# Filling products moved ahead of the second block's query product, and a third buffer for the index numbers

## The chip, the cores and the metric

The kernel runs on one core of a Trainium2 chip. The metric is the device time of one execution in microseconds (us). The core's engines work side by side, each in the order of its own queue: TensorE (PE) multiplies matrices, VectorE (DVE) and ScalarE (ACT) do element-wise work and copies, GpSimd (POOL) does element-wise work and issues the transfers that gather or scatter rows by index, and SyncE (SP) issues most other transfers (DMAs). An engine waits for another one, or for a transfer, at a semaphore.

## The reference

A gated linear attention over 4 batches, 8 heads, 768 tokens and head size 48 feeds a mixture of 8 experts in which every token goes to one expert.

```python
for t in range(S):                                # attention, per batch and head
    state = alpha[:, :, t, :, None] * state + np.einsum('bhd,bhe->bhde', k[:, :, t], v[:, :, t])
    y[:, :, t] = np.einsum('bhd,bhde->bhe', q[:, :, t], state)
...
for s in range(S):                                # experts, per batch; x is y, 384 wide
    fresh_e = int(np.argmax(logits[b, s]))
    if s == 0 or local_gate[b, s] < 0.5:
        e = fresh_e
    else:
        e = prev_e if prev_e >= 0 else fresh_e
    ...
    h = np.maximum(x[b, s] @ w1[e], 0.0)          # w1[e]: 384 x 1024
    out[b, s] = p[e] * (h @ w2[e])                # w2[e]: 1024 x 384
```

## The kernel before

**The attention stage** takes 24 blocks of 128 tokens, two chunks of 64 each, in one loop over `i`. Blocks 0 to 3 are the first blocks of the four batches. For block `i` DVE computes running products of the gate and their reciprocals (`scan1`, `scan2`; the tiles `A` and `sf`), two blocks ahead of use, and POOL multiplies query and key with them. PE multiplies keys with queries (`pm`, into the bank `pz`), transposes the keys (`kt`, tile `kp`, copied to `kk` by ACT), multiplies queries with the state (`qm`, into `py`), keys with values (`um`, into `up`), and masked scores with values (`ym`, onto `py`). DVE masks the scores (`mask`, tile `pq`) and adds up the state (`sums`, tile `st`). The order of the work on each engine is the order in which the code is written, since every call is pinned to it. In iteration `i` PE's order is `pm(i)`, `kt(i)`, transposes of the finished rows of block `i-2`, `qm(i-1)`, `um(i)`, `ym(i-1)`. The query product `qm(i-1)` reads the state that `sums(i-1)` writes, and DVE's order is `sums(i-1)`, `mask(i)`, `scan1(i+2)`, `scan2(i+2)`.

**Filling products** are products of a tile of zeros, `dz`, with itself. Their results are read by nobody. `dense(DN0)` issues 56 ahead of the loop, and `um` issues `DN + DN1 * (i < 2)` into unread columns of `up`, ahead of its own work: eight for block 0 and eight for block 1.

**The expert stage** works in jobs. The last attention blocks run beside the first expert's jobs `a` and `b`; then come seven jobs `r0` to `r6`, one for each other expert by rank, with up to 512 rows in slices of up to 128. A job has a first layer (`gemm1`: eight groups of nine products into the banks of tile `h`; ACT and DVE turn each group into the parts `hh` and `hl`), a second layer (`gemm2`: 24 products a slice into `yp`, scaled by DVE into `yo`), and a scatter of each slice's rows to the output (`store`). Three banks take the groups of `h` in turn, so the fourth group waits until `hl` of the first has been computed. When job n starts, `numbers()` computes for job n+1 the index numbers `ix` of its rows, on DVE, from `pr`, a row of the lists picked by rank; the gathers of job n+1 and its scatters read them. The tile `ix` has two buffers there, so the numbers of job n+1 go where those of job n-1 stood, whose scatters have been issued as its slices were finished.

Of the kernel before, what the change touches and what calls it, by code (L numbers as in the profile page):

```python
# [10 lines left out]
I32 = mybir.dt.int32  # L11
# [44 lines left out]
NL = 5  # L56
NW = 3
DN0 = 56
DN = 0
DN1 = 8  # L60


# [10 lines left out]
def gla_moe(ctx, tc, akq, vw, vn, wg, w1, w2, cst, tok, out):  # L73
# [30 lines left out]
    v_, s_, g_, t_, y_ = (Engine(e) for e in (nc.vector, nc.scalar, nc.gpsimd, nc.tensor, nc.sync))  # L104
# [105 lines left out]
    class Job:  # L210
# [14 lines left out]

        def numbers(self, more=None):

            self.ix = self.sp.tile([128, 2, self.ns], I32, tag="ix", bufs=2, name=f"ix_{self.nm}")
            if callable(self.first):
                self.pr = self.first()  # L230
                v_.tensor_tensor(self.ix, self.pr[:, 1:3, 0:self.ns], back.unsqueeze(2).broadcast_to([128, 2, self.ns]), ALU.add)
            else:
                w = slice(self.first, self.first + self.ns)
                self.pr = lists[:, :, w]
                v_.tensor_tensor(self.ix, self.pr[:, 1:3], back.unsqueeze(2).broadcast_to([128, 2, self.ns]), ALU.add)
# [88 lines left out]
        def store(self, yo, yp, s):  # L324
            P = self.ways[s].stop - self.ways[s].start
            v_.tensor_scalar_mul(yo, yp, self.pr[0:P, 0, s:s + 1])
            apart(outs, g_.indirect_dma_start(out=out, out_offset=bass.IndirectOffsetOnAxis(
                ap=self.ix[0:P, 0, s:s + 1], axis=0), in_=yo, in_offset=None,
                bounds_check=NTOK - 1, oob_is_err=False))
# [5 lines left out]
    with ac:  # L335
# [4 lines left out]
        py = pa.tile([128, 2, 512], F32, tag="y", name="py")  # L340
# [6 lines left out]
        dz = ap.tile([128, 256], F32R, bufs=1, name="dz")  # L347
# [56 lines left out]
        def qm(i):  # L404

            d = blk[i]
            q = d["q"].rearrange("p (h t) -> p h t", h=HP)
            for hp in range(HP):
                for (e, c) in ((0, 0), (1, 1), (0, 1), (1, 0)):
                    if c == 0 and i < G:  # L410
                        continue
                    r = slice(0, 48) if e else slice(64, 112)
                    t_.matmul(py[c * C:(c + 1) * C, e, hp * D:(hp + 1) * D], lhsT=q[r, hp, c * C:(c + 1) * C],
                              rhs=d["s3"][r, c, hp, :], start=(hp == 0), stop=False, skip_group_check=True)
            r = slice(C if i < G else 0, 128)
            s_.copy(seen[r].rearrange("p (e h) -> p e h", e=2), py[r, :, 0:HP * D:D])

        def half(i):
            vt = blk[i]["vt"]
            s_.copy(vt[0:64, 0, :], vt[0:64, 1, :])  # L420
# [35 lines left out]
        def kt(i):  # L456
            k = blk[i]["k"].rearrange("p (h t) -> p h t", h=HP)
            kp = pp.tile([128, HP, R], F32, tag="kp", name=f"kp_{i}")
            for hp in range(HP):
                t_.transpose(kp[:, hp, :], k[:, hp, :], ident[0:R, 0:R])  # L460
            kk = ap.tile([128, HP, R], F32, tag="kk", name=f"kk_{i}")
            s_.copy(kk, kp)
            blk[i]["kk"] = kk

        def pm(i):

            d = blk[i]
            k = d["k"].rearrange("p (h t) -> p h t", h=HP)
            q = d["q"].rearrange("p (h t) -> p h t", h=HP)
            pe = pz  # L470
            for hp in range(HP):
                for (par, c) in ((0, 0), (1, 1), (0, 1), (1, 0)):
                    w = slice(c * C, (c + 1) * C)
                    r = slice(0, 48) if par else slice(64, 112)
                    t_.matmul(pe[c * C:(c + 1) * C, par, hp * C:(hp + 1) * C], lhsT=k[r, hp, w], rhs=q[r, hp, w],
                              start=True, stop=True)
            d["pe"] = pe

        def mask(i):
            d = blk[i]  # L480
            pq = ap.tile([128, 2, HP, C], F32, tag="pq", bufs=2, name=f"pq_{i}")
            v_.tensor_tensor(pq, d["pe"][:, :, 0:HP * C].rearrange("p e (h t) -> p e h t", h=HP),
                             cc("tri")[:, 0:C].unsqueeze(1).unsqueeze(1).broadcast_to([128, 2, HP, C]), ALU.mult)
            d["pq"] = pq

        def state0(i):

            d = blk[i]
            if i < G:
                d["s3"] = ap.tile([R, 3, HP, D], F32, tag="st", bufs=G + 1, name=f"st_{i}")  # L490
            else:
                d["s3"] = st["S", i % G]

        def um(i):

            d = blk[i]
            kk, vt = d["kk"], d["vt"]
            uw = pp.tile([128, 512], F32, tag="up", name=f"up_{i}")
            for _ in range(DN + DN1 * (i < 2)):
                t_.matmul(uw[:, 384:512], lhsT=dz[:, 0:128], rhs=dz[:, 0:128], start=True, stop=True)  # L500
            d["up"] = uw[0:R, 0:2 * CW].rearrange("p (h c d) -> p c h d", c=2, h=HP)
            for hp in range(HP):
                n = slice(2 * hp * D, 2 * (hp + 1) * D)
                t_.matmul(uw[64:112, n], lhsT=kk[:, hp, 64:112], rhs=vt[:, :, 2 * hp * D:(2 * hp + 1) * D],
                          start=True, stop=True)
                t_.matmul(uw[0:64, n], lhsT=kk[:, hp, 0:64], rhs=vt[:, :, (2 * hp + 1) * D:(2 * hp + 2) * D],
                          start=True, stop=True)

        def sums(i):
            d = blk[i]  # L510
            s3 = d["s3"]
            n = 2 if i + G < NB else 1
            if i < G:
                v_.tensor_copy(s3[:, 1:1 + n], d["up"][:, 0:n])
                return
            v_.tensor_tensor(s3[:, 1:1 + n], d["up"][:, 0:n], s3[:, 0].unsqueeze(1).broadcast_to([R, n, HP, D]), ALU.add)
# [24 lines left out]
        def xt(i):  # L541
            XR = blk[i]["XR"]
            xp = pp.tile([128, DM], F32, tag="xp", name=f"xp_{i}")
            for k in range(3):
                t_.transpose(xp[:, k * 128:(k + 1) * 128], XR[:, k * 128:(k + 1) * 128], ident)
            if i % G == 0:
                st["xx"] = ap.tile([128, G, 3, 128], F32, tag="xx", bufs=1, name=f"xx_{i // G}")
            s_.copy(st["xx"][:, i % G].rearrange("p k t -> p (k t)"), xp)
            del blk[i]
# [282 lines left out]
        def other(kind=None):  # L832

            for r in list(steps):
                if r[1] == "h" or kind and r[1] not in (kind, None):
                    continue
                r[1] = next(r[0], 0)
                if r[1] == 0:
                    steps.remove(r)
            if kind in ("s", "p", "g"):  # L840
                return
            flush()
# [102 lines left out]
        for i in range(NB):  # L945
            other("s")
            half(i)
            if i:
                sums(i - 1)
            state0(i)  # L950
            pm(i)
            kt(i)
            mask(i)
            other("d")
            if i > 1:
                store(i - 2)
                xt(i - 2)
            if i:
                qm(i - 1)
            um(i)  # L960
            other("p")
            for r in early_rows:
                for _ in r:
                    pass
            early_rows[:] = []
            if i:
                carry(i - 1)
            if i + 2 < NB:
                scan1(i + 2)
                scan2(i + 2)  # L970
            if i + 2 >= NB:
                behind_route()
            next(st_up, None)
            other("g")
            if i:
                ym(i - 1)
            if i > NB - 3:
                unit()
            if i > 1:
                logit(i - 2)  # L980
            if i + 2 < NB:
                ends(i + 2)
            if i + 4 < NB:
                load(i + 4)
            if i and i + NP - 1 < NB:
                load_v(i + NP - 1)
            if gathers:
                if gathers[0] == 1:
                    early_rows.append(ja.trans())
                gathers[0] += 1  # L990
            if i in SPLITS:
                EW.split(SPLITS.index(i), pieces)
            wanted[0] += i in LOADS
            while wanted[0] and len(EW.raw) - NW < EW.cast:
                wanted[0] -= 1
                EW.load()
        drained[0] = True
        behind_route()
        i = NB - 1
# [305 lines left out]
```

## Time and profile before

| | |
|---|---|
| median of three runs | 398.15 us (397.67 to 400.63) |
| the profiled execution | 396.98 us, span 395.1 us |
| busy, share of the span | PE 94%, DVE 63%, ACT 45%, POOL 42% |
| granted clock of PE, mean | 0.989 |
| bytes moved | 63.30 MB, mean 160 GB/s |

Times in rows are microseconds from the start of the span. [...] A row of a timeline gives start and duration, engine, operation, output and inputs; `x8` merges eight instructions of one kind, and a bracket tells how long the engine stood idle before it and what it waited for. Nearly all rows name line 97, since one helper issues every instruction; the names of the tiles tell them apart.

### The profile page before, as it was taken

What the parts mean: (1) busy time and instruction counts of PE and PEld (TensorE: products, weight loads), DVE (VectorE), ACT (ScalarE), POOL (GpSimd) and SP (SyncE); (2) the same over time, 40 slices, a digit from 0 to 9 for tenths busy, and PEclk for the clock granted to TensorE, in tenths of its full rate; (3) what the DMA queues carried; (4) which work ended last, traced back from release to release, by engine and by line L of the source; (5) the groups of instructions that cost most, each with busy time, mean ns of one, the idle gap of its engine ahead of it and who ended that gap; (6) DMA issues with size and microseconds to landing.
All of it is one profiled execution on the core that took longest, in us unless ns stands there. A gap on an engine that the chain in (4) does not pass through costs nothing.

```text
span 395.1 us, 11436 instructions
## 1 busy us (share of the span) xinstructions
PE 373.2 (94%) x4535; PEld 342.9 (87%) x4535; DVE 247.2 (63%) x565; ACT 177.5 (45%) x452; POOL 165.8 (42%) x226
## 2 busy tenths in 40 slices
PE   7899989989999999999999999999999899999990
PEld 7787877877888899998899899999899799999990
DVE  8889989999875577765552562554445655564410
ACT  2266766687785530543522541542452451643200
POOL 7548756656688114344321712422432432612010
PEclk9999999999999999999999999999999999999997
DMA  8979899986746001684441472394197174461010
GB/s 233 212 208 232 232 263 246 254 236 167 219 127 181 26 22 37 210 278 139 149 154 51 146 204 100 85 338 169 33 308 258 30 263 147 149 194 59 1 41 7
DMA packets 27002, 63.30 MB, mean 160 GB/s; under 512 B 4964, under 2 KB 11446, under 8 KB 26946
## 3 DMA queue, kind: packets, MB, share of 16 engines
q1 hardware_dynamic: 23218, 52.37, 46.0%
q0 software_dynamic: 3584, 10.04, 7.2%
q8 instruction: 36, 0.59, 0.6%
q14 instruction: 20, 0.16, 0.1%
q10 hardware_dynamic: 144, 0.14, 0.1%
HBM read 53.09 MB, written 10.04 MB: 160 GB/s over the span
## 4 chain that ended last, share of the span: by engine, by line
PE 68%; issue 12%; DVE 11%; ACT 3%; POOL 2%; DMA 2%; SPq 0%; POOLq 0%; DVEq 0%; ACTq 0%
PE h_r L97 20%; PE yp_r L97 19%; PE py L97 6%; PE pz L97 4%; PE up L97 3%; DVE sf L97 3%; DVE A L97 3%; PE yp_b L97 2%; PE tp_r L97 2%; PE h_a L97 2%; PE lq L97 2%; POOL out L97 1%; DMA ld<-akq 1%; PE yp_a L97 1%; PE kp L97 1%
## 5 line engine op out<-in xcount | busy, mean ns | idle before, releaser
L97 POOL DMA_INDIRECT out<-yo_r,ix_r x25 | 24.9, 995 | 121.6 <-DVE yo_r L97 97.0
L97 PE MATMUL yp_r<-w2h_r,hh_r 128*128 128x384 f32 (+2 forms) x184 | 63.7, 346 | 0.0
L97 PE MATMUL yp_r<-w2h_r,hl_r 128*128 128x384 f32 (+2 forms) x184 | 61.9, 336 | 0.0
L97 PE MATMUL yp_r<-w2l_r,hh_r 128*128 128x384 f32 (+2 forms) x184 | 61.9, 336 | 0.0
L97 PE MATMUL h_r<-xh_r,w1h_r 128*128 128x384 f32 (+5 forms) x168 | 60.1, 358 | 1.2 <-DVE hl_r L97 1.2
L97 PE MATMUL h_r<-xl_r,w1h_r 128*128 128x384 f32 (+5 forms) x168 | 59.7, 356 | 0.0
L97 PE MATMUL h_r<-xh_r,w1l_r 128*128 128x384 f32 (+5 forms) x168 | 59.7, 355 | 0.0
L97 DVE SCALAR_TENSOR_TENSOR hl_r<-h_r,hh_r 128x384 fp32r<-128x384 f32 (+3 forms) x56 | 32.7, 585 | 32.6 <-ACT hh_r L97 32.2
L97 ACT ACTIVATE hh_r<-h_r 128x384 fp32r<-128x384 f32 (+3 forms) x56 | 28.7, 513 | 44.9 <-PE h_r L97 44.8
L97 DVE TENSOR_TENSOR_SCAN sf<-ld,sf,zp 112x128 f32<-112x128 f32 x96 | 38.3, 462 | 0.9
L97 POOL DMA_INDIRECT xg_r<-xd,ix_r x25 | 28.1, 1126 | 19.8 <-issue 9.0
L97 PEld LDWEIGHTS h_r<-xh_r,w1h_r 128*128 128x128 f32 x168 | 31.6, 188 | 4.7 <-DVE hl_r L97 1.5
L97 POOL TENSOR_TENSOR ld<-ld,A 112x512 f32<-112x512 f32 x24 | 28.4, 1182 | 15.7 <-DVE A L97 12.3
L97 PEld LDWEIGHTS yp_r<-w2h_r,hh_r 128*128 128x128 f32 (+2 forms) x184 | 34.2, 186 | 0.4
L97 PEld LDWEIGHTS yp_r<-w2l_r,hh_r 128*128 128x128 f32 (+2 forms) x184 | 34.3, 186 | 0.3
L97 PEld LDWEIGHTS yp_r<-w2h_r,hl_r 128*128 128x128 f32 (+2 forms) x184 | 34.2, 186 | 0.2
L97 POOL TENSOR_TENSOR ld<-ld,sf 112x512 f32<-112x512 f32 x24 | 28.4, 1184 | 13.9 <-DVE sf L97 12.7
L97 PEld LDWEIGHTS h_r<-xl_r,w1h_r 128*128 128x128 f32 x168 | 31.6, 188 | 2.1 <-DVE xl_r L97 0.3
L97 PEld LDWEIGHTS h_r<-xh_r,w1l_r 128*128 128x128 f32 x168 | 31.6, 188 | 1.9
L97 DVE TENSOR_TENSOR_SCAN A<-ld,zp 112x260 f32<-112x260 f32 x48 | 30.8, 683 | 2.7
L97 ACT CAST xh_r<-tp_r 128x384 fp32r<-128x384 f32 (+4 forms) x25 | 11.3, 456 | 45.1 <-PE tp_r L97 44.0
L97 DVE TENSOR_TENSOR xl_r<-tp_r,xh_r 128x384 fp32r<-128x384 f32 (+4 forms) x25 | 13.1, 525 | 26.0 <-ACT xh_r L97 26.0
(215 smaller groups left out, 783.0 us busy)
## 6 DMA issues: line engine op xcount, KB each, us to landing
rw_r<-w SPq DMA_DIRECT2D x21, 512.0 KB, 4.1
rw_r<-w SPq DMA_DIRECT2D x28, 384.0 KB, 4.0
ld<-akq SPq DMA_DIRECT2D x44, 192.0 KB, 4.7
vt<-vn SPq DMA_DIRECT2D x24, 192.0 KB, 3.7
xd<-XR SPq DMA_DIRECT2D x24, 192.0 KB, 3.8
ld<-akq SPq DMA_DIRECT2D x44, 97.7 KB, 4.2
wf_r<-w SPq DMA_DIRECT2D x8, 384.0 KB, 5.9
rw_a<-w SPq DMA_DIRECT2D x3, 512.0 KB, 5.4
```

Of the source, the lines that this page charges most:

```text
L97: r = f(*a, **k)
```

## The change

The constant `DN` becomes 9 and is used in another place: the loop issues nine filling products into unread columns of `py` in the iteration `i == 1`, ahead of `qm(0)`. `um` issues its eight for block 0 alone. The tile `ix` gets a third buffer.

```diff
-DN = 0
+DN = 9
 DN1 = 8
...
-            self.ix = self.sp.tile([128, 2, self.ns], I32, tag="ix", bufs=2, name=f"ix_{self.nm}")
+            self.ix = self.sp.tile([128, 2, self.ns], I32, tag="ix", bufs=3, name=f"ix_{self.nm}")
...
             uw = pp.tile([128, 512], F32, tag="up", name=f"up_{i}")
-            for _ in range(DN + DN1 * (i < 2)):
+            for _ in range(DN1 * (i < 1)):
                 t_.matmul(uw[:, 384:512], lhsT=dz[:, 0:128], rhs=dz[:, 0:128], start=True, stop=True)
...
                 xt(i - 2)
+            for _ in range(DN * (i == 1)):
+                t_.matmul(py[:, 1, 256:384], lhsT=dz[:, 0:128], rhs=dz[:, 0:128], start=True, stop=True)
             if i:
                 qm(i - 1)
             um(i)
```

PE's order in iteration 1, before (`st_240` is the state of block 0, `kk_328` the transposed keys of block 1):

```order
L97 MATMUL pz<-ld_118 64x64 x15
L97 MATMUL kp_323<-cs,ld_118 128x112 [waits PE_49]
L97 MATMUL kp_323<-cs,ld_118 128x112 x3
L97 MATMUL py<-st_240,ld_117 64x48 [waits DVE_49]
L97 MATMUL py<-st_240,ld_117 64x48 x7
L97 MATMUL up_341<-dz 128x128 [waits PE_49]
L97 MATMUL up_341<-dz 128x128 x7
L97 MATMUL up_341<-vt_110,kk_328 48x96 [waits DMAHW0_49,Activation_49]
```

and with the change:

```order
L97 MATMUL pz<-ld_118 64x64 x15
L97 MATMUL kp_323<-cs,ld_118 128x112 [waits PE_49]
L97 MATMUL kp_323<-cs,ld_118 128x112 x3
L97 MATMUL py<-dz 128x128 x9
L97 MATMUL py<-st_240,ld_117 64x48 [waits DVE_49]
L97 MATMUL py<-st_240,ld_117 64x48 x7
L97 MATMUL up_350<-vt_110,kk_328 48x96 [waits DMAHW0_49,Activation_49]
```

The filling products stand ahead of the product that waits for DVE, and wait for nothing themselves; the state products follow the query product directly.

DVE's order at the start of job r4, where the numbers of job r5 are computed, before (`DMASW` are semaphores of POOL's transfers, eight lanes in turn):

```order
L97 TENSOR_SCALAR yo_r_2_4943<-yp_r_2_4912,pr_4306 128x384 [waits PE_49]
...
L97 TENSOR_REDUCE pr_4970<-al_4968 128x12 [waits DVE_49]
L97 TENSOR_TENSOR ix_r_4967<-pr_4970,back 128x6 [waits DMASW4_49,DMASW5_49,DMASW2_49,DMASW6_49,DMASW1_49,DMASW7_49,DMASW0_49,DVE_49]
L97 SCALAR_TENSOR_TENSOR hl_r_0_4984<-h_r_0_4973,hh_r_0_4983 128x384 [waits Activation_49]
L97 TENSOR_TENSOR w2l_r_5_4988<-rw_r_5_4821,w2h_r_5_4987 128x768 [waits DMAHW3_49,Activation_49]
```

and with the change:

```order
L97 TENSOR_SCALAR yo_r_2_4944<-yp_r_2_4913,pr_4307 128x384 [waits DMASW2_49,PE_49]
...
L97 TENSOR_REDUCE pr_4971<-al_4969 128x12 [waits DVE_49]
L97 TENSOR_TENSOR ix_r_4968<-pr_4971,back 128x6 [waits DMASW6_49,DMASW5_49,DMASW7_49,DMASW4_49,DVE_49]
L97 SCALAR_TENSOR_TENSOR hl_r_0_4985<-h_r_0_4974,hh_r_0_4984 128x384 [waits Activation_49]
L97 TENSOR_TENSOR w2l_r_5_4989<-rw_r_5_4822,w2h_r_5_4988 128x768 [waits DMAHW3_49,Activation_49]
```

The numbers name four lanes of POOL's transfers in place of seven, and `yo` of the slices ahead names a lane that the numbers named before. The order of DVE's instructions is the same.

## Rows read from the trace of the kernel before

**Rows 1.** The page: busy time of PE, and the granted clock in 40 slices.
```profile
PE 373.2 (94%) x4535; PEld 342.9 (87%) x4535; DVE 247.2 (63%) x565; ACT 177.5 (45%) x452; POOL 165.8 (42%) x226
PEclk9999999999999999999999999999999999999997
```

**Rows 2.** Windows of half a us: length, busy times, granted clock, DMA share, GB/s.
```profile
17.50:18.00 0.50, 0.50 (x6) 0.50 (x6) 0.50 (x1) 0.47 (x3) 0.00 (x0) 1.00 1.07 207
...
18.50:19.00 0.50, 0.50 (x7) 0.45 (x8) 0.37 (x2) 0.14 (x1) 0.24 (x1) 0.50 0.98 211
...
21.50:22.00 0.50, 0.50 (x40) 0.50 (x37) 0.00 (x0) 0.16 (x1) 0.35 (x1) 1.00 0.41 78
```

**Rows 3.** Timeline of PE, blocks 0 to 2.
```profile
12.39 1.09 PE L97 MATMUL up<-dz 128*128 128x128 f32 x8
...
14.84 0.60 PE L97 MATMUL kp<-cs,ld 112*128 112x112 f32 x4
16.70 0.67 PE L97 MATMUL py<-st,ld 48*64 48x48 f32 x16 [1.26 <-DVE st L97]
17.30 1.32 PE L97 MATMUL up<-dz 128*128 128x128 f32 x8
18.55 1.55 PE L97 MATMUL up<-vt,kk 128*48 128x96 f32 x16
...
22.20 0.60 PE L97 MATMUL kp<-cs,ld 112*128 112x112 f32 x4
```

**Rows 4.** Timeline of DVE, the same stretch and one block more.
```profile
20.52 0.53 DVE L97 COPY st<-up 112x384 f32<-112x384 f32 x1
22.33 0.69 DVE L97 TENSOR_TENSOR pq<-pz,cs 128x512 f32<-128x512 f32 x1 [1.28 <-PE pz L97]
...
26.74 0.68 DVE L97 TENSOR_TENSOR pq<-pz,cs 128x512 f32<-128x512 f32 x1
```

**Rows 5.** Timelines of ACT and POOL, the other inputs of blocks 1 and 2.
```profile
15.48 0.53 ACT L97 COPY kk<-kp 128x448 f32<-128x448 f32 x1 [0.55 <-PE kp L97]
...
16.28 1.18 POOL L97 TENSOR_TENSOR ld<-ld,sf 112x512 f32<-112x512 f32 x1 [0.73 <-DVE sf L97]
```

**Rows 6.** Timeline of PE, the next iterations.
```profile
23.07 0.67 PE L97 MATMUL py<-st,ld 48*64 48x48 f32 x16
23.67 0.88 PE L97 MATMUL up<-vt,kk 128*48 128x96 f32 x16
...
26.02 0.61 PE L97 MATMUL kp<-cs,ld 112*128 112x112 f32 x4
...
26.89 0.67 PE L97 MATMUL py<-st,ld 48*64 48x48 f32 x16
...
31.28 0.67 PE L97 MATMUL py<-st,ld 48*64 48x48 f32 x16 [0.51 <-DVE st L97]
```

**Rows 7.** Who waited for the scatters of the output: us, times.
```profile
DVE ix_r L97: 11.5, 5
```

**Rows 8.** Page, costliest groups (busy, mean ns, idle before); timeline of PE, job r4.
```profile
L97 PE MATMUL h_r<-xh_r,w1h_r 128*128 128x384 f32 (+5 forms) x168 | 60.1, 358 | 1.2 <-DVE hl_r L97 1.2
...
311.87 0.34 PE L97 MATMUL h_r<-xh_r,w1l_r 128*128 128x384 f32 x1
313.38 0.44 PE L97 MATMUL h_r<-xh_r,w1h_r 128*128 128x384 f32 x1 [1.17 <-DVE hl_r L97]
```

**Rows 9.** Timeline of DVE, start of job r4.
```profile
310.34 0.25 DVE L97 TENSOR_REDUCE pr<-al 128x12 f32<-128x96 f32 x1
312.57 0.17 DVE L97 TENSOR_TENSOR ix_r<-pr,back 128x6 int32<-128x6 f32 x1 [1.97 <-DMA out<-yo_r,ix_r]
```

**Rows 10.** A window of 6 us in the expert stage, columns as in rows 2.
```profile
316.00:322.00 6.00, 6.00 (x36) 6.00 (x35) 3.41 (x5) 3.34 (x7) 3.85 (x3) 1.00 0.75 236
```

**Rows 11.** Who waited for whom, 0 to 160 us: total, times, longest (PEld: weight loads).
```profile
PEld py L97 <- issue: 5.8, 26, 1.0
```

**Rows 12.** A window of 4 us in the attention stage, columns as in rows 2.
```profile
84.00:88.00 4.00, 2.63 (x69) 2.08 (x69) 3.78 (x15) 3.06 (x9) 1.95 (x3) 1.00 0.99 299
```

## The prediction

> **What bounds the kernel now.** I read the page first, the shares of the engines and the row of the granted clock [rows 1]. TensorE (PE) is busy for 94% of the span, and the clock's row, a mean over slices of 9.9 us, shows nothing of the clock; cut into half microseconds, the start of the kernel does [rows 2]. [...] What PE did before the fall is in its rows of that stretch [rows 3]: after the transposes of block 1 (14.84 + 0.60 = 15.44 us) it stood 1.26 us, until VectorE (DVE) had copied the state `st` that the query product of block 0 reads; then came that product, the eight filling products, and block 1's state products at the low level. Who paid is in DVE's rows [rows 4]: the mask `pq` of block 2 began at 22.33 us after 1.28 us of standing for PE's scores `pz`, and one block later the same mask came 4.41 us after it, with DVE standing nowhere. So from 22.33 us on DVE is the bound of this stage, and PE waits for it again (0.51 us for `st` at 31.28 us) [rows 6]. Whatever the mask at 22.33 us gains, DVE's chain takes along.
>
> The expert stage is bound by PE: between 316 and 382 us eleven windows of 6 us in a row each show 6.00 us of PE [rows 10]. The list of waits on the scatters says that the index numbers `ix_r` stood five times, 11.5 us in all, until an earlier scatter had landed [rows 7]. All but one of the five were free for PE: over all seven rank jobs its first-layer products `h_r` stood 1.2 us [rows 8]. That one is in job r4: DVE had `pr` ready at 310.59 us, `ix_r` started at 312.57 [rows 9], and PE stood 1.17 us for the `hl_r` queued behind it [rows 8].
>
> **The change, part by part.** *Filling products.* Eight leave the place ahead of block 1's state products, and nine come ahead of block 0's query product, into columns of `py` that nobody reads; the first eight, of block 0, stay. Eight such products took 1.09 us at the high level [rows 3], so nine take at most 9/8 of that, 1.23 us. They wait for nothing: they begin behind the transposes and are over by 15.44 + 1.23 = 16.67 us, inside PE's wait, which ended at 16.70. The ninth is thus free, as the eight were not: they stood between 17.30 and 18.55 us. Now the query product still starts at 16.70 (its `st` comes from DVE) and the state products at 17.30 instead of 18.55. Their other input, `kk` of block 1, was copied by 15.48 + 0.53 = 16.01 us; the scores behind them need keys that POOL finished at 16.28 + 1.18 = 17.46 us [rows 5].
>
> From the start of the state products to the end of the scores PE needs 26.02 - 23.67 = 2.35 us at the high level [rows 6], and 22.20 - 18.55 = 3.65 us in the stretch that was mostly low [rows 3]. So the scores are ready at 17.30 + 2.35 = 19.65 us if the clock holds, and at 20.95 us if it falls all the same. Late next is DVE itself: it sums the state from 20.52 us for 0.53, to 21.05, and the mask comes behind that [rows 4]. Either way DVE's whole idle time of **1.28 us** goes, from 22.33 back to 21.05, and no more, since DVE then has none left to give. From below the term is nothing (a first rival); a loss would need the nine to run past 16.70 us by more than the 21.05 - 19.65 = 1.4 us that the scores are early, and even at 1.25 us for eight, partly at the low level [rows 3], nine take 1.41 us and end at 16.85. No DMA is moved, and none is passed on SP's or POOL's queue.
>
> *Index numbers.* A third buffer adds 32 bytes a partition and no instruction. Job n's numbers now go where job n-3's stood, whose scatters were issued a whole job earlier. The order shows waits of `ix_r` on DMA lanes still; worked out from the order of GpSimd's (POOL's) transfers, they are those of gathers long landed. Waits on scatters now stand at `yo_r`, for the scatter four stores back. In r4 `ix_r` can follow `pr` at about 310.6 us and release PE 313.38 - 312.57 = 0.81 us later, at 311.4, before PE has issued the last product ahead of the stall (311.87) [rows 8, 9]. So the whole **1.17 us** goes. In the four others DVE and the gathers come about 2 us earlier and PE gains nothing; POOL's gathers and SP's weight loads start earlier with them, and I put that at nothing either way, since behind them no PE wait for weights or rows shows in these windows. The bounds of this term are 0 and 1.2 us, the page's sum [rows 8].
>
> Both gains lie on the path: nothing between 22 and 316 us runs by a clock of its own, each wait there follows a producer. The sum is 1.28 + 1.17 = 2.45 us. The profiled execution took 396.98 us (span 395.1 and 1.9 around it) and would take 394.53. The median shown, 398.15, lies 1.17 above it; there I forecast 398.15 - 2.45 = **395.7 us**.
>
> One thing is not in this sum. PE's query products stand 26 times for a cause that the trace does not name, 5.8 us in all, up to 1.0 us each [rows 11]. Work that starts 1.3 us earlier may meet these otherwise; I take 1.5 us either way for the range, about a quarter.
>
> **The rivals.** *(a) The clock does not fall in most executions of the kernel before.* Then the state products there start at 17.30 + 1.09 = 18.39 us, the scores are ready by 18.39 + 2.35 = 20.74, before DVE wants them at 21.05, and the filling term is nothing: 398.15 - 1.17 = 397.0. For it: PE stood longer elsewhere without one: between 84 and 88 us it worked 2.63 of 4 us at 1.00 [rows 12]. Against: the one execution that can be read has the fall, and it ran 1.17 us under the median. [...] No trace here shows a second execution. I give it 0.2.
>
> *(b) The clock stays low.* The early iterations leave PE short gaps in front of each query product (0.51 us at 31.28 [rows 6]), and the gap in front of block 1's query product, new, has no filling: 21.1 us when `st` is there, while PE gets there at 17.30 + 26.89 - 23.67 = 20.5 us. If the level falls there and does not come back, an iteration of PE, 26.89 - 23.07 = 3.82 us [rows 6], takes 1.55 to 1.76 times that (3.65 to 2.35 above; 1.55 against 0.88 us for the state products [rows 3, 6]), about 6.3 us, over DVE's 4.41 by 1.9. It decides from the second such iteration: 395.7 + 3.8 = 399.5, slower than before; four make 403.3. Against it: gaps of that size, and the larger one at 84 us, stood at 1.00. I give it 0.06.
>
> *(c) The wait of `ix_r` stays*, because the DMA lanes it still names count later transfers than I take them for: 398.15 - 1.28 = 396.9. Chance 0.06.
>
> *(d) The unnamed stalls fall better:* 395.7 - 1.5 = 394.2 or less. Chance 0.1.
>
> **How the numbers follow.** The forecast has the remaining 0.58 and the time, 395.7. The range reaches down to 394.0 for (d) and up to 397.8, over (a) and (c) with 0.8 us for the stalls; (b) and half of (d) stay out. A measurement of this kernel can tell about 1% from no change, 4 us: faster means under 394.2, slower over 402.1. Faster is (d) in the main, 0.1; slower is the longer half of (b) and a little for what I don't see, 0.04; the rest, 0.86, is within 1%, though I expect a gain.
>
> **What would show it.** Right: nine products on `py` between about 15.3 and 16.7 us and no wait over 0.3 us behind them; the granted clock at 1.00 from 14 to 24 us; DVE's mask of block 2 at about 21.0 us with no idle time ahead of it; the `ix_r` rows following `pr` within 0.3 us; no PE wait at r4's fourth group of `h_r`; PE's last product some 2.4 us earlier. Wrong: a clock of 0.50 somewhere in 18 to 30 us with DVE waiting for `pz`; `ix_r` still ended by a DMA; or both gains in their places and a new idle time on PE or DVE between 40 and 170 us that eats them.

## The result, and the profile after

| | before | after |
|---|---|---|
| median | 399.11 us (396.45 to 400.63, 14 runs) | 394.06 us (392.7 to 402.18, 14 runs) |
| ratio of the two | | 0.9905, 95% interval 0.9878 to 0.9931 |
| the profiled execution | 396.98 us, span 395.1 | 392.89 us, span 391.1 |
| granted clock of PE, mean | 0.989 | 0.992 |

Ratios leave out executions over 1.5% above the fastest of their kernel, such as the one of 402.18 us. A second comparison gave 395.38 us (393.44 to 398.64, 12 runs) and a ratio of 0.9924 [0.9891, 0.9957]. The forecast was 395.7, a gain of 2.45 us; the two ratios are gains of about 3.8 and 3.0 us, and the lower ends of their intervals 2.8 and 1.7.

**The start.** PE's timeline of the changed kernel, blocks 0 to 2, beside [rows 3]:

```profile
11.45 1.09 PE L97 MATMUL up<-dz 128*128 128x128 f32 x8
...
13.90 0.60 PE L97 MATMUL kp<-cs,ld 112*128 112x112 f32 x4
14.27 1.20 PE L97 MATMUL py<-dz 128*128 128x128 f32 x9
15.76 0.67 PE L97 MATMUL py<-st,ld 48*64 48x48 f32 x16 [0.29 <-DVE st L97]
16.36 0.88 PE L97 MATMUL up<-vt,kk 128*48 128x96 f32 x16
...
18.71 0.60 PE L97 MATMUL kp<-cs,ld 112*128 112x112 f32 x4
20.16 0.67 PE L97 MATMUL py<-st,ld 48*64 48x48 f32 x16 [0.52 <-DVE st L97]
```

The nine stand in the wait and leave 0.29 us of its 1.26. The state products follow the query product directly and take 0.88 us in place of 1.55. In the profile before, the granted clock was 1.00 until 18.0 us, 0.50 until 21.5 and 1.00 again; the windows in which it fell and rose, beside [rows 2] (columns: window, length, busy us of PE, weight loads, DVE, ACT and POOL, granted clock as a share of the full one, DMA share, GB/s):

```profile
18.00:18.50 0.50, 0.50 (x4) 0.43 (x3) 0.50 (x2) 0.50 (x3) 0.00 (x0) 0.54 0.83 193
...
21.00:21.50 0.50, 0.50 (x19) 0.50 (x18) 0.05 (x1) 0.00 (x0) 0.50 (x1) 0.54 0.95 197
```

The same stretch lies 1 us earlier here, and shows 1.00 throughout:

```profile
16.50:17.00 0.50, 0.50 (x16) 0.50 (x14) 0.50 (x1) 0.47 (x3) 0.01 (x1) 1.00 0.92 198
17.50:18.00 0.50, 0.50 (x26) 0.50 (x26) 0.40 (x2) 0.20 (x1) 0.18 (x1) 1.00 1.06 234
18.50:19.00 0.50, 0.50 (x17) 0.43 (x10) 0.50 (x3) 0.50 (x3) 0.50 (x1) 1.00 0.91 200
```

DVE's timeline beside [rows 4]; the mask of block 2 has no idle time ahead of it:

```profile
11.21 0.69 DVE L97 TENSOR_TENSOR pq<-pz,cs 128x512 f32<-128x512 f32 x1 [0.27 <-PE pz L97]
...
19.57 0.53 DVE L97 COPY st<-up 112x384 f32<-112x384 f32 x1
20.02 0.68 DVE L97 TENSOR_TENSOR pq<-pz,cs 128x512 f32<-128x512 f32 x1
24.42 0.69 DVE L97 TENSOR_TENSOR pq<-pz,cs 128x512 f32<-128x512 f32 x1
```

That mask comes 2.31 us earlier than before (22.33), but not all of it is the filling: the masks of blocks 0 and 1 are 0.94 us earlier already (11.21 and 15.62, before 12.15 and 16.56), ahead of every instruction that the change moved. The 0.94 us lie in the opening, 56 products that both kernels issue. In PE's timeline they are one row, of the kernel before:

```profile
2.34 9.12 PE L97 MATMUL pz<-dz 128*128 128x240 f32 x56 [2.34 <-DVE dz L97]
```

and of the changed kernel:

```profile
2.34 8.18 PE L97 MATMUL pz<-dz 128*128 128x240 f32 x56 [2.34 <-DVE dz L97]
```

So the filling gained 2.31 - 0.94 = 1.37 us here. From block 2 to block 23, whose mask is at 125.64 us (before 127.92), the lead stays between 2.28 and 2.32.

**The expert stage.** DVE's timeline at the start of r4, beside [rows 9]:

```profile
308.04 0.25 DVE L97 TENSOR_REDUCE pr<-al 128x12 f32<-128x96 f32 x1
308.32 0.17 DVE L97 TENSOR_TENSOR ix_r<-pr,back 128x6 int32<-128x6 f32 x1
308.52 0.56 DVE L97 SCALAR_TENSOR_TENSOR hl_r<-h_r,hh_r 128x384 fp32r<-128x384 f32 x1
```

The numbers follow `pr` after 0.03 us instead of 1.98; no wait on a scatter is left in the list of [rows 7]. PE's products at the place of the stall in [rows 8], where the third group of r4 ends and the fourth begins:

```profile
309.40 0.33 PE L97 MATMUL h_r<-xl_r,w1h_r 128*128 128x384 f32 x1
309.58 0.33 PE L97 MATMUL h_r<-xh_r,w1l_r 128*128 128x384 f32 x1
309.75 0.33 PE L97 MATMUL h_r<-xh_r,w1h_r 128*128 128x384 f32 x1
309.92 0.33 PE L97 MATMUL h_r<-xl_r,w1h_r 128*128 128x384 f32 x1
```

They start 0.17 to 0.18 us apart throughout. By the starts of PE's first product of each layer, all seven jobs up to the second layer of r6 take 369.06 - 176.63 = 192.43 us against 373.05 - 178.87 = 194.18, and r4's first layer 12.59 against 14.08. That is 1.75 us, of which r4 has 1.49. With the 1.37 of the filling and the 0.94 of the opening, which is no gain of the change, it makes 4.06 us; the spans of the pair differ by 4.0. Another part was not forecast: r0's first layer takes 16.51 us against 16.95, r5's 12.48 against 12.71, with no wait gone. The costliest groups by shape (busy us, mean ns | idle before), before:

```profile
L97 PE MATMUL h_r<-xh_r,w1h_r 128*128 128x512 f32 x24 | 9.5, 396 | 0.0
L97 PE MATMUL h_r<-xh_r,w1h_r 128*128 128x384 f32 x48 | 16.4, 342 | 1.2 <-DVE hl_r L97 1.2
```

and after:

```profile
L97 PE MATMUL h_r<-xh_r,w1h_r 128*128 128x512 f32 x24 | 9.3, 390 | 0.0
L97 PE MATMUL h_r<-xh_r,w1h_r 128*128 128x384 f32 x48 | 16.1, 336 | 0.0
```

### The profile page after: what moved, and what is told of

Its sections match the earlier page's. It is cut to its first block, busy times and chain, and to the rows that moved or that the text cites. A ratio compares the mean times of both kernels' runs of the same rounds, so it can differ in the third digit from the quotient of the medians.

```text
span 391.1 us, 11445 instructions
## 1 busy us (share of the span) xinstructions
PE 370.5 (95%) x4536; PEld 340.9 (87%) x4536; DVE 248.5 (64%) x565; ACT 177.9 (45%) x452; POOL 166.4 (43%) x226
## 4 chain that ended last, share of the span: by engine, by line
PE 64%; DVE 15%; issue 12%; DMA 3%; POOL 2%; ACT 2%; SPq 0%; DVEq 0%; POOLq 0%; ACTq 0%
PE h_r L97 20%; PE yp_r L97 19%; PE py L97 5%; DVE sf L97 4%; DVE A L97 4%; PE pz L97 3%; DMA ld<-akq 2%; PE yp_b L97 2%; PE tp_r L97 2%; PE up L97 2%; PE h_a L97 2%; DVE pq L97 2%; POOL out L97 2%; PE yp_a L97 1%; DVE st L97 1%
```

## The experiments

Three theories on the filling: the fall of the clock comes of the unfilled wait and the nine prevent it (A); the eight products cost time because they stand behind the wait, and taking them away is enough (B); the fall comes in some executions and not in others, whatever is filled (C). Two on the third buffer: its gain is the waits (D), or also where the tiles behind it stand in memory (E).

**The third buffer alone**, `e1`.

```diff
-... tag="ix", bufs=2, name=f"ix_{self.nm}")
+... tag="ix", bufs=3, name=f"ix_{self.nm}")
```

> The kernel before with the third buffer for ix and nothing else. Theory 1 (two separate terms, each removes one wait; the rest of the measured gain is where the clock rose in the opening): ix_r follows pr at once, the 1.17 us stand of PE in job r4 is gone, and the ratio is 0.997 (398 to 399 becomes about 397.5). Theory 2 (most of the measured gain comes from the index numbers, through earlier gathers and weight loads as well): ratio 0.992 or less. The mask of block 2 still waits for PE where the clock falls near 18 us.

Measured: 397.24 us, before 399.24, ratio 0.994 [0.9903, 0.9977]; from r0's first to r6's second layer 192.49 us. The buffer has its full gain alone. At the start it is the kernel before, and its clock falls like it, to 0.50 from 18.5 to 21.5 us (PE, then DVE):

```profile
16.91 0.67 PE L97 MATMUL py<-st,ld 48*64 48x48 f32 x16 [1.26 <-DVE st L97]
...
18.56 1.55 PE L97 MATMUL up<-vt,kk 128*48 128x96 f32 x16
```

```profile
22.53 0.69 DVE L97 TENSOR_TENSOR pq<-pz,cs 128x512 f32<-128x512 f32 x1 [1.27 <-PE pz L97]
```

**The filling alone**, `e2`: the change with the old number of buffers.

```diff
-... tag="ix", bufs=3, name=f"ix_{self.nm}")
+... tag="ix", bufs=2, name=f"ix_{self.nm}")
```

> The change with two buffers for ix: only the filling products move. Theory 1: the idle time of DVE ahead of the mask of block 2 (1.28 us) is gone, PE still stands 1.17 us in r4; ratio 0.9965 (1.4 us). If the unfilled gap of the kernel before costs more executions a low clock later on, the ratio is lower, down to 0.993. Theory 2: ratio 0.998 to 1.

Measured: 398.05 us, ratio 0.996 [0.9928, 0.9992]. The mask of block 2 (21.22 us) follows that of block 1 (16.82) after 4.40 us, the steady period, and the stall in r4 is back. Within their intervals the two parts add up: 0.994 times 0.996 is 0.990.

**No filling for block 1**, `e3`: as `e2`, and

```diff
-DN = 9
+DN = 0
```

> Two buffers for ix, the eight filling products of block 1 left out and the nine not put in. If taking the eight from the path is what helps, the state products start right behind the query product, the scores are ready 21.0 us at the latest even at the low level, and the ratio is that of the filling alone (0.9965). If the nine are needed to hold the clock, the granted clock falls to 0.50 within 2 us behind the gap in most executions and stays low for over 3 us, DVE waits for pz, and the ratio is 0.999 or above.

Measured: 397.53 us, ratio 0.9947 [0.9916, 0.9978], not to be told from `e2`. Masks 4.40 us apart (15.80, 20.20), and a granted clock of 1.00 from 14 to 25 us though the wait was unfilled. That one profile speaks against A.

**Filling in both places**, `e4`: as `e2`, and

```diff
-            for _ in range(DN1 * (i < 1)):
+            for _ in range(DN1 * (i < 2)):
```

> Two buffers for ix, nine filling products ahead of the query product and the eight ahead of the state products as well. If the clock is what matters, it holds at 1.00, the scores are ready about 20.7 us (less what the opening is earlier), before DVE wants them, and the ratio is that of the filling alone (0.9965). If the path is what matters, DVE waits about 0.3 us or more for pz and the ratio is 0.998 or above.

Measured: 397.76 us, ratio 0.9963 [0.9933, 0.9993]. DVE shows that the eight products behind the wait, 1.11 us long, cost it nothing at a granted clock of 1.00: the mask of block 2 comes 4.41 us after that of block 1 (15.82), with no idle time ahead of it.

```profile
20.23 0.68 DVE L97 TENSOR_TENSOR pq<-pz,cs 128x512 f32<-128x512 f32 x1
```

So B in its simple form falls too: here the eight cost nothing at 1.00, while in `e1`, where the clock fell, DVE stood 1.27 us behind them.

**A shorter opening**, `e5`: the change with

```diff
-DN0 = 56
+DN0 = 46
```

> The change with 46 filling products ahead of the loop in place of 56. Theory 1 (the 0.94 us that the profiled executions differ by at block 0 is where the clock rose while those 56 ran: 8.18 us of them against 9.12): ten fewer end 0.9 us earlier, DVE's mask of block 0 waits 0.3 us or less for pz in place of 0.27 to 1.47, and the ratio is 0.9985 to 0.998 of the change, some 0.989 of the kernel before. Rival: the clock rises later or falls in the first blocks, since fewer products run there, and the ratio is that of the change (0.9905) or above it; the trace then shows a granted clock of 0.50 behind 10 us.

Measured: 394.52 us (6 runs) against 399.93, ratio 0.9899 [0.9846, 0.9951]: not to be told from the change. In its profile the 46 took 8.13 us, as long as 56 in the changed kernel's (8.18), so in this execution nothing was saved.

**Placement alone**, `e6`: the kernel before, with a longer tile of which the old part is used. The tiles behind it, `xh`, `xl` and `hh` among them, stand 64 bytes further in each partition, as they do with the third buffer (32 bytes for the buffer itself, and the tiles behind it move by 64); the order and the waits stay.

```diff
-... self.sp.tile([128, 2, self.ns], I32, tag="ix", bufs=2, name=f"ix_{self.nm}")
+... self.sp.tile([128, 3, self.ns], I32, tag="ix", bufs=2, name=f"ix_{self.nm}")[:, 0:2]
```

> The kernel before with two buffers for ix that are each half as large again, so that every later tile of the pool stands 64 bytes further on, as with the third buffer, and each engine's order and waits are those of before. If the pace of the first-layer products hangs on where their tiles stand: r0's come 0.227 us apart in place of 0.233 (16.5 us for its first layer, not 16.95) and r5's 0.173 in place of 0.177, while the 1.17 us stand in r4 stays. If the pace comes with the waits of ix: 0.233 and 0.177 as before.

Measured, in one execution: 395.7 us, span 393.9. Its costliest groups, as above:

```profile
L97 PE MATMUL h_r<-xh_r,w1h_r 128*128 128x384 f32 x48 | 16.3, 339 | 1.2 <-DVE hl_r L97 1.2
...
L97 PE MATMUL h_r<-xh_r,w1h_r 128*128 128x512 f32 x24 | 9.4, 390 | 0.0
```

The stall of r4 is there, and yet the products of 512 columns have the changed kernel's 390 ns. r0's first layer took 16.49 us and r5's 12.48, r4's 14.06; all jobs together 193.91 against 194.18. So E: 1.75 us are some 1.5 of waits and 0.2 to 0.3 of placement.

**The kernel before, again**, `e7`.

> The kernel before, a second execution with a profile. Theory 1 (the unfilled gap invites a fall, and where it comes is chance): if the 56 products of the opening end near 10.5 us, the fall may come elsewhere in 14 to 100 us or be missing; near 11.5 us, it comes at about 18 us again and DVE waits 1.2 us or more for pz of block 2. Without a fall, DVE's wait ahead of that mask is 0.3 us or less.

Measured: 395.82 us, span 394.0. PE, then DVE:

```profile
2.34 8.10 PE L97 MATMUL pz<-dz 128*128 128x240 f32 x56 [2.34 <-DVE dz L97]
...
15.68 0.67 PE L97 MATMUL py<-st,ld 48*64 48x48 f32 x16 [1.26 <-DVE st L97]
16.27 1.11 PE L97 MATMUL up<-dz 128*128 128x128 f32 x8
17.31 0.88 PE L97 MATMUL up<-vt,kk 128*48 128x96 f32 x16
```

```profile
19.49 0.53 DVE L97 COPY st<-up 112x384 f32<-112x384 f32 x1
19.94 0.68 DVE L97 TENSOR_TENSOR pq<-pz,cs 128x512 f32<-128x512 f32 x1
```

The same unfilled wait of 1.26 us, the same eight behind it, and no fall (the granted clock is 1.00 from 14 to 25 us): DVE does not wait, and the filling term is nothing. This is the prediction's rival (a) in an execution.

**No filling, again**, `e8`: the kernel of `e3`.

> The kernel without any filling for block 1, a second execution with a profile. If the path is what matters, DVE has no wait for pz ahead of the mask of block 2 even where the granted clock falls at 17 to 19 us (the scores are then ready at or before the state sum ends); if the low level matters by itself, a fall there comes with a wait of 0.5 us or more.

Measured: 396.83 us, span 395.0. Late opening (9.14 us), unfilled wait, no fall (1.00 from 14 to 25 us), no wait of DVE:

```profile
20.53 0.53 DVE L97 COPY st<-up 112x384 f32<-112x384 f32 x1
20.98 0.68 DVE L97 TENSOR_TENSOR pq<-pz,cs 128x512 f32<-128x512 f32 x1
```

**The change again**, `e9`, and **the change without the nine**, `e10`, on one chip. The edit of `e10`, with the third buffer kept:

```diff
-DN = 9
+DN = 0
```

> The change once more, beside the next kernel on one chip. Theory 1 (third buffer 1.7 us, of which 1.5 is the stand in r4, and a filling term that is 0 or 1.3 us by where the clock falls): 2 to 3.2 us under the kernel before, ratio 0.992 to 0.995. Theory 2 (the two together keep the clock up over the whole kernel): ratio 0.990 or less and a mean granted clock of 0.991 or more in the middle execution, where the kernel before has 0.985.

> The change without its nine filling products (none for block 1 at all, three buffers for ix). If the nine do nothing but stand out of the way: the ratio of the change itself, and a mean granted clock like its. If they hold the clock: 1.3 us or more above the change, ratio 0.994 or above, and a middle granted clock lower by 0.003 or more.

Measured: 395.38 us, ratio 0.9924 [0.9891, 0.9957], and 395.77 us, ratio 0.9934 [0.9898, 0.997]; before 398.82. The two medians are 0.4 us apart, where holding the clock was to be worth 1.3. The nine products can't be shown to be worth anything beside the removal of the eight. `e9` had the latest opening of all (9.51 us) and no fall.

The profile of `e10`, of its execution of 402.17 us, does have the fall, though nothing stands behind the unfilled wait: the granted clock is 0.84 between 18.0 and 18.5 us and 0.50 from there to at least 25.0, and its mean over the execution is 0.971. PE, then DVE:

```profile
17.45 0.88 PE L97 MATMUL up<-vt,kk 128*48 128x96 f32 x16
...
23.62 1.55 PE L97 MATMUL up<-vt,kk 128*48 128x96 f32 x16
```

```profile
21.12 0.69 DVE L97 TENSOR_TENSOR pq<-pz,cs 128x512 f32<-128x512 f32 x1
...
26.78 0.69 DVE L97 TENSOR_TENSOR pq<-pz,cs 128x512 f32<-128x512 f32 x1 [1.02 <-PE pz L97]
```

The mask of block 2 comes 4.41 us after that of block 1 (16.71), as without a fall. The mask of block 3 comes 5.66 us later, 1.26 beyond the period. So here, with the eight gone, the fall did not delay block 2, but it lasted into the next iteration and was paid there.

**The kernel before, a third profile**, `e11`.

> The kernel before, a third execution with a profile: if the 56 products of the opening end near 11.5 us, a granted clock of 0.50 from about 18 us and a wait of DVE for pz of block 2 of 1.2 us; if they end near 10.5 us, neither.

Measured: 397.8 us, span 396.0, mean clock 0.982. The fall is here, earlier and longer than in the first profile. Windows of half a us, the first with the fall and the last:

```profile
16.50:17.00 0.50, 0.50 (x12) 0.45 (x8) 0.36 (x3) 0.14 (x1) 0.38 (x1) 0.81 1.06 306
17.00:17.50 0.50, 0.50 (x4) 0.50 (x4) 0.50 (x2) 0.47 (x3) 0.00 (x0) 0.50 0.87 172
...
23.00:23.50 0.50, 0.50 (x4) 0.50 (x4) 0.50 (x1) 0.02 (x1) 0.00 (x0) 0.50 0.78 116
23.50:24.00 0.50, 0.50 (x5) 0.38 (x3) 0.35 (x3) 0.12 (x1) 0.00 (x0) 0.87 0.96 352
```

PE and DVE pay for it:

```profile
16.72 1.92 PE L97 MATMUL up<-dz 128*128 128x128 f32 x8
18.56 1.55 PE L97 MATMUL up<-vt,kk 128*48 128x96 f32 x16
```

```profile
22.93 0.69 DVE L97 TENSOR_TENSOR pq<-pz,cs 128x512 f32<-128x512 f32 x1 [2.22 <-PE pz L97]
```

The eight filling products ran at the low level, 1.92 us, all of them ahead of the scores that DVE waited 2.22 us for. From the mask of block 1 (15.98) to that of block 2 are 6.95 us, 2.55 more than the period of 4.40.

**The change without the nine, a profile**, `e12`: the kernel of `e10`.

> One profile of the change with DN = 0: the eight filling products of block 1 are gone and none stand ahead of the query product, so the PE wait of 1.26 us there stays unfilled. Theory (what counts is that the eight products left the path behind the query product): even if the clock falls at this wait, the state products start 0.6 us after the query product; at the high level DVE's mask of block 2 begins without idle time, 4.4 us after the mask of block 1. Rival (the nine are what keeps the clock up): the clock falls to 0.50 somewhere in 16 to 18 us, as in two of three profiles of the kernel before, and the mask of block 2 comes 5.0 us or more after that of block 1, with DVE waiting for pz. Two earlier profiles without filling there had no fall; a third without makes three of three. The expert jobs r0 to r6 as in the change: 192.4 us from the first layer of r0 to the second layer of r6.

Measured: 393.94 us, span 392.1, clock 0.995; r0 to r6 192.42 us. No fall, and the mask of block 2 waits for nothing:

```profile
15.68 0.67 PE L97 MATMUL py<-st,ld 48*64 48x48 f32 x16 [1.30 <-DVE st L97]
16.28 0.88 PE L97 MATMUL up<-vt,kk 128*48 128x96 f32 x16
```

```profile
19.49 0.53 DVE L97 COPY st<-up 112x384 f32<-112x384 f32 x1
19.94 0.68 DVE L97 TENSOR_TENSOR pq<-pz,cs 128x512 f32<-128x512 f32 x1
```

**Taken together**, all profiles by the order of the work around that wait:

| order in iteration 1 | executions | fall that begins between 16 and 19 us | block 2's mask, us beyond the period |
|---|---|---|---|
| wait unfilled, eight behind it | before, `e1`, `e11`; `e6`, `e7` | in the first three | 1.37, 1.36, 2.55; 0, 0 |
| wait unfilled, none behind it | `e10`; `e3`, `e8`, `e12` | in `e10` | 0; 0, 0, 0 |
| wait filled with nine | after, `e2`, `e4`, `e5`, `e9` | none | 0 in all five |

That the fall comes in some executions and not in others (C) is shown for the kernel before, whose own three profiles differ, and for the change without the nine (`e10` beside `e12`). That the new order prevents the fall is not shown: at a chance of 4 in 9, which the unfilled waits of both kinds show together, five executions without one come up in about 1 of 20 cases, and three of the four without any filling have none either. Nor does the opening decide it alone: falls followed openings of 9.12, 9.33, 8.54 and 9.27 us, and none followed 8.25, 8.10, 9.14 and 9.51.

## Why the prediction was right, and where only in part

**The forecast.** It said a gain of 2.45 us that a measurement can hardly tell from no change. The two gains are where it put them, but the gain was larger than forecast, and the range, 394.0 to 397.8, held the time, 394.06, only at its edge. The medians differ by 5.05 us, more than either ratio says; part of that is the draw of executions, as the second comparison's 395.38 shows. The forecast was also counted from the median of three runs, 398.15; from that of fourteen, 399.11, it would be 396.66.

**The filling term, 1.28 us.** In the profiled pair it measured 1.37. The steps held: nine products ahead of the wait's end, the state products directly behind the query product, the clock at 1.00 from 14 to 24 us, DVE with no idle time left. They came 1 us earlier than written because of the opening, which the prediction took as fixed. But the term was read from one execution and stands for a mean: over the five profiles with the order of before it is (1.37 + 1.36 + 2.55 + 0 + 0) / 5 = 1.06 us, with the largest twice the forecast. The step that DVE "then has none left to give" beyond 1.28 thus held for that execution alone; in `e11` DVE had stood 2.22.

**Rival (a)**, that the clock does not fall in most executions of before, had 0.2. Its mechanism is real: in `e7` and `e6` the eight products ran at 1.00 (1.11 us), and the mask started when DVE came to it, as the rival's sum has it. "Most" is not shown: one of the three profiles of the kernel before was free of it, two of five with `e1` and `e6`. The fall of the kernel before came at 18.0 us in the first profile, between 16.5 and 17 in `e11`, and nowhere between 14 and 25 us in `e7`. One kernel thus met it at different places or not at all, so the term should have been a mean over executions and not the size of one.

**What the nine do.** The prediction costed them at nothing, hidden in the wait, and that holds (0.29 us of the wait were left). A gain of their own was neither claimed nor found (`e10` beside `e9`, and `e3` beside `e2`).

**The index term, 1.17 us, was too small.** r4's first layer lost 1.49. The stall as a gap in the row of busy time is 1.17, but the starts around it are 313.38 - 311.87 = 1.51 us apart where 0.17 is usual [rows 8], which is 1.34; the products after the restart are slower by the rest (the first is 0.44 us long beside 0.34). A stall on a saturated engine is to be read from start to start. The other four waits gained nothing, as said; rival (c), that `ix_r` keeps waiting, is refuted by the row at 308.32 us. To this comes the placement, 0.2 to 0.3 us net, which the prediction took for no change ("adds 32 bytes a partition and no instruction").

**The unnamed stalls, 1.5 us either way.** In the profiled pair they changed nothing: from the mask of block 2 to that of block 23 are 105.59 us before and 105.62 after. Between executions the same stretch took 105.59 to 107.91 us (`e3`), 105.84 and 106.99 in the two other profiles of the kernel before, 106.23 in the other of the change. So this term was about the right size and belongs to the execution, not to the change, though how much of the difference is those stalls was not separated. The time lies where rival (d) was put (394.2 or less), but its mechanism does not show in these profiles.

**Rival (b)**, a clock that stays low, had 0.06. In none of the five profiles with the nine was there a fall in this stretch; `e2` has one between 86.5 and 90 us. But its mechanism was met without the nine: in `e10` the fall lasted into the next iteration and DVE's chain lost 1.26 us there (the rival put 1.9 on each such iteration).

**The sum.** 1.06 for the filling on average and 1.75 for the buffer are 2.8 us, 0.7%. The intervals of `e1` (0.2 to 1.0%), `e2` (0.1 to 0.7%) and the second comparison (0.4 to 1.1%) hold their parts; the first comparison's, 0.7 to 1.2%, holds it at its edge. What may lie beyond 2.8 us was not found. The mean granted clock of the runs in the ratios may point to the start: its median is 0.985 and 0.986 for the kernel before in the two large comparisons, 0.992 for the change and 0.989 for `e1`. But the changed kernel shows 0.50 behind PE's last product too (it starts at 381.39 us; the clock is 0.50 from 385.0 to the end of the span at 391.1), so the mean does not say where.

## What to carry to other kernels

In these runs filling products cost nothing inside a wait (nine took 1.20 us of it and left 0.29), and behind one eight took 1.11 us at a granted clock of 1.00, where the mask lost nothing by them, and up to 1.92 us where it fell to 0.50 and the mask came up to 2.55 us late; the first gain is to take them off the path, and whether they also hold the clock up must be shown by leaving them out, in several executions. Take at least three profiles before sizing a term that rests on a fall of the clock: the same kernel lost 1.37, 0 and 2.55 us in three. Read a stall of the bounding engine from start to start of the instructions around it, and see whether a buffer added ahead of matmul operands has moved them (here by 64 bytes in each partition, for 0.2 to 0.3 us).

## What the runs showed of the hardware that was not expected

**Placement.** Operands 64 bytes further in each partition changed the spacing of products at a granted clock of 1.00: 512 columns from 0.233 to 0.227 us (r0), 384 columns from 0.177 to 0.173 (r5), and in r1's first layer the other way (15.10 to 15.19 us). `e6` shows 0.227 us (r0) and 0.173 (r5) without any other change. Which of the moved tiles does it was not tried.

**The opening.** In the kernel before 19 of its products start between 3 and 7 us and 18 between 9 and 11, so about 4.75 and 9 to a us. The windows, columns as above, count every product that touches them (7 and 11) and show the granted clock at 1.00 throughout:

```profile
6.00:7.00 1.00, 1.00 (x7) 1.00 (x7) 0.96 (x4) 0.14 (x1) 0.95 (x1) 1.00 1.08 284
...
8.00:9.00 1.00, 1.00 (x11) 1.00 (x11) 1.00 (x2) 0.00 (x0) 1.00 (x1) 1.00 1.05 295
```

and of the changed kernel:

```profile
6.00:7.00 1.00, 1.00 (x12) 1.00 (x11) 0.96 (x4) 0.14 (x1) 0.95 (x1) 1.00 1.08 294
```

The pace rose between 7.5 and 8 us in the one and between 5.5 and 6 in the other, and the 56 products took 8.06 to 9.51 us over the thirteen profiles that issue 56. The granted clock in the rows does not show this step, the count of products does; why it comes where it does stays open.
